# A banded attention and gated MLP kernel: a fourth staging buffer, 4 KB rows for two weights, and new lengths and margins in the planner that orders its instructions

## The chip, the cores and the metric

One core of one Trainium2 chip. The metric is the device time of one launch in microseconds. The kernel before takes 775.3 us (median of 3 runs, 772.66 to 777.56).

## What is computed

Attention over 4 batches, 8 heads, 768 positions and head width 64. A position sees itself and the 127 positions before it, and the first 4 positions of the sequence (the "sinks"). The result, 3072 rows of 512, goes through a gated MLP with 1536 hidden units. All is float32.

```python
scores = scale * np.matmul(q, k.transpose(0, 1, 3, 2))
keep = is_sink | in_window
scores = np.where(keep, scores, -1000000000.0)
scores = scores - np.max(scores, axis=-1, keepdims=True)
a = np.exp(scores)
a = a / (np.sum(a, axis=-1, keepdims=True) + 1e-09)
x = np.matmul(a, v)                      # then heads side by side: 3072 x 512
...
gate = 1.0 / (1.0 + np.exp(-(x @ w_gate)))
val = x @ w_val
return (gate * val @ w_out).astype(np.float32)
```

The three weights arrive as 64-bit floats.

## The kernel before, in words

**Tiling.** Attention runs in 96 units: a unit u is one head of one block of 256 query positions (`attend`, line 892). For each it forms scores on TensorE (PE), masks them and takes the maximum on VectorE (DVE), exponentiates on ScalarE (ACT), normalises (on GpSimd, ACT or DVE), turns the weights with PE transposes, cuts them into two triangular parts on GpSimd (POOL; `split`, `rest_of`) and multiplies by v. The first 20 units (`PLAIN`) use plain float32 matmuls of two passes; later ones split numbers into a high and a low part (tiles `hi`, `kl`, `vhl`) and use the faster fp32r form.

**The MLP** runs over 8 chunks of positions (`CHUNKS`), each over 12 slices f of 128 hidden units. Chunk 0 uses plain float32 (`feed_whole`, 1414), chunks 1 to 3 `feed_plain` (1515), and chunks 4 to 7, two blocks each, `feed_pair` (1561), which saves products by sums of blocks. Up products go to the PSUM tiles `m`, the down products to tiles `o` and `a`; between them stand `th`, `gh` and `gl` on ACT, DVE and POOL (`gated`, 1489).

**Weights.** `weights` (1307) calls `decode` (1256) 36 times: SP loads a 512 KB piece of 64-bit numbers into a staging tile `wst` (pool tag with `B_wst` = 3 buffers; the mask builder takes one of them first), and two ACT and two DVE instructions make float32 of it. `halves` (1334) and `thirds` (1343) split the weights in high and low parts; low parts are written to DRAM (`wlo_d`, `spare`, 1319) and read back slice by slice (`fetch`, 1462, tile `lo`, 8 buffers).

**The order of everything** is made at build time by a planner (`class Plan`, `run`, line 353). Each operation has a priority, the tiles it reads and writes, and one or more ways: an engine and a length in ns. `run` plays the program through with these lengths. Whenever an engine is free it gives it the first ready operation by priority; so the lengths decide which engine takes an operation that has several ways, and in what order each engine's instructions stand. Between the end of an operation and the readiness of one that needs it the planner puts `LAT` = 180 ns (line 411); PE first takes operations whose inputs are at least `SURE` = 600 ns old (`SURE_D` = 1200 ns for a landed DMA). Where PE has nothing ready in the first 130 us, `run` puts a filler, a 128x128 matmul of the identity (`warm`, 807; `m<-ident` in the trace; line 537). On the chip each engine then goes through its list in this order and waits on semaphores; the planner's lengths themselves are not waited for. All DMAs are issued by one queue, SP.

**The end.** The general branch for other masks is skipped by a jump. `hint` (1685) puts branch hints for PE, DVE and SP in their lists, called in `last_slice` (1641, the call is line 1665).

Line 620 is the helper that issues every planned instruction, so nearly all rows have L620.

Of the kernel before, what the change touches and what calls it, by code (L numbers as in the profile page):

```python
# [29 lines left out]
CROWD = 1.0  # L30
# [4 lines left out]
BACKV = 0.0  # L35
FLIP = 1
HOLD = 0.6
HELD = 800000.0
GAP = 2.0
# [3 lines left out]
THIRDS = 130000.0  # L43
CROWDED = 350000.0
PLAIN = 20
SINKP = -2.0
SCALP = -0.5
SKSWAP = 0
WHOLE = 1
DN1 = 36  # L50
DS1 = 8.0
DR1 = 0.2
DS2 = 18.0
DR2 = 0.3
KS1 = 16.0
KR = 0.9
KS2 = 25.0
XP = -900.0
ALT = 1
LAT = 180.0  # L60
BULK = 620.0
ISSUE = 550.0
SURE = 600.0
SURE_D = 1200.0
FREE = 150.0
NEXT = dict(PE=0.0, V=60.0, A=60.0, G=60.0, Q=0.0)
# [21 lines left out]
B_lo = 8  # L88
B_w2 = 2
B_wst = 3  # L90
# [222 lines left out]
class Plan:  # L313
# [39 lines left out]
    def run(self, warm, fill_ns, fill):  # L353
# [37 lines left out]
        while events:  # L391
            now = events[0][0]
            while events and events[0][0] <= now:
# [14 lines left out]
                for x in o.after:  # L408
                    x.before -= 1
                    same = len(x.ways) == 1 and x.ways[0][0] == on  # L410
                    x.ready = max(x.ready, now + (NEXT[on] if same else LAT))
                    if on != "PE":
                        x.sure = max(x.sure, now + LAT + (SURE_D if o.dma else SURE))
                    if not x.before:
                        n += 1
                        heapq.heappush(events, (x.ready, n, ("ready", x, None)))
            for e in free:
                if free[e] > now:
                    continue
                held = []  # L420
                unsure = [] if e == "PE" else None
                while waiting[e] or unsure:
# [18 lines left out]
                    if unsure is not None and (  # L441
                        o.sure > now
                        or any(slots[k][v - 1][1] + LAT + SURE > now for k, v in need.items())
# [51 lines left out]
                    if through:  # L495
                        ns += max(0.0, port - now - LEAD)
                        port = now + ns + (70.0 if e == "V" else 0.0)
# [26 lines left out]
                    for x in o.after:  # L524
                        x.todo -= 1
                        x.due = max(x.due, end + LAT)
# [23 lines left out]
def kernel(  # L550
# [13 lines left out]
    w_gate, w_val, w_out = (  # L564
        w.bitcast(I32).rearrange("r (c w) -> r c w", w=2) for w in (w_gate, w_val, w_out)
    )
    B, H, S, D = v.shape
    DM, DF, _ = w_gate.shape
    DO = w_out.shape[1]
    NC = DM // 128  # L570
    NF = DF // 128
# [63 lines left out]
    def act(cols, psum=False):  # L635
        return 120 + 0.9 * cols

    def pool(cols):
        return Port(170 + 2.17 * cols)
# [199 lines left out]
    WLO, LOADS, GROUPS, DECODED, READY, READY2 = (Fixed(None) for _ in range(6))  # L839

    def sinks(b, u):
        if not b:
# [7 lines left out]
            for t, x in enumerate(VS0):  # L850
                for y in range(2):
                    o = 64 * y + NS * t
                    dma(
                        u + 0.5, 91.0, lambda x=x, y=y, o=o: Q.dma_start(
# [8 lines left out]
        for o in range(0, 128, NS):  # L863
            dma(
                u, 91.0, lambda o=o: Q.dma_start(
                    out=raw()[o : o + NS], in_=v[b, :, 0:NS, :].rearrange("h p d -> p h d"),
                ), [READY2], [(raw, o)] + [VSHL[b, i] for i in range(2) if b and (b, i) in VSHL],
# [10 lines left out]
    def load(u, b, h, t0, T, prev, L, vraw, vin, qkT, plain):  # L878
# [4 lines left out]
            u, 0.75 * n * R / D, lambda: Q.dma_start(out=qkT()[0:R, 0:n], in_=qk[b, h, 0:R, c0 : c0 + n]),  # L883
# [3 lines left out]
            u, 100.0 * L, lambda: Q.dma_start(  # L887
# [4 lines left out]
    def attend(u, b, h, t0, T, XR):  # L892
# [44 lines left out]
        for t in range(T):  # L937
# [28 lines left out]
            def exp(t=t):  # L966
# [5 lines left out]
            plan.op(u, [("PE", 10 + (4 * n / 2.4 + 6 if plain else 2 * mac(n)), scores)], qk_reads, [sc, (P, t)], busy=0.5 if plain else 0.9)  # L972
            plan.op(
                u, [("V", 260 if first else 535, top)],
                [sc, (MASKS, 3), (MASKS, min(t0 + t, 2))], [sc, (P, t), (NEGM, (u, t))],
            )
            plan.op(u, [("A", 410, exp)], [], [(P, t), (rs, t)])
# [19 lines left out]
        def mul():  # L997
            for t in range(T):
# [4 lines left out]
                ("A", 200, lambda: A.activation(  # L1003
                    out=rs()[:, 0:T], in_=rs()[:, 0:T], func=AF.Copy, scale=1.0, bias=1.0e-9
                )),
                ("G", Port(213), guard(G)), ("V", Port(100), guard(V)),
# [3 lines left out]
            u, [("V", 110, lambda: V.reciprocal(out=rs()[:, 0:T], in_=rs()[:, 0:T]))], [], [rs]  # L1010
        )
        plan.op(u, [("G", Port(660), share), ("A", 720, mul), ("V", Port(555), scale)], [rs], [P])

        if not plain:
# [11 lines left out]
                u, [("V", 180, lambda: V.transpose(  # L1026
# [10 lines left out]
                u, [("G", Port(610), spread(G)), ("V", two(W), spread(V))], [turned, OWN], [sk]  # L1037
# [35 lines left out]
        plan.op(u, [("PE", 30 + (T + plain) * 110, turn)], [P], [tp, wt], busy=0.45)  # L1073
# [745 lines left out]
```

## Time and profile before

| | |
|---|---|
| runs | 775.3 us median (772.66, 775.3, 777.56) |
| the profiled execution, its own time | 774.19 us |
| its span, first to last instruction | 772.5 us |
| instructions | 16296 |
| TensorE clock granted, mean | 0.998 |
| DMA bytes | 185.57 MB, 240 GB/s over the span |

The page counts a matmul as busy from its start to a modelled end, and matmuls overlap: a wait shorter than what the last matmul's record still covers does not show as idle time. Rows with "[1.63 <-DMA x]" tell the idle time of the engine before the instruction and what ended it.

### The profile page before, as it was taken

To read this page: it belongs to the slowest core of one execution; us is meant where nothing else is said; L and a number is where in the kernel's file an instruction comes from. 1 tells how busy PE (TensorE), PEld (TensorE's weight loads), DVE (VectorE), ACT (ScalarE), POOL (GpSimd) and SP (SyncE) were. 2 spreads that over 40 slices of the span, in tenths; PEclk is the share of its full clock that TensorE was granted. 3 is DMA by queue.
4 is the path that set the end of the run, shared out by engine and by line. 5 is a ranking of instruction groups with operands and counts; after the bars stand their busy time and mean duration, and the time that the engine had idled before them with its cause. 6 is when DMAs were issued, how large, how long until landed. Compare 5 with 4: busy or idle time off the path is not lost.

```text
span 772.5 us, 16296 instructions
## 1 busy us (share of the span) xinstructions
PE 749.1 (97%) x4986; PEld 674.9 (87%) x4986; DVE 607.5 (79%) x1782; ACT 472.0 (61%) x1338; POOL 506.1 (66%) x647
## 2 busy tenths in 40 slices
PE   7999999999999999999999999999999999999995
PEld 6866777998989999989999988999999999999995
DVE  5979988996999999969988889778999884433333
ACT  7879888765765777737666665457776652322221
POOL 3654676887999999937777977557976855321210
PEclk9999999999999999999999999999999999999999
DMA  6898987999999877677767777867697655677662
GB/s 165 222 297 250 323 263 234 376 307 311 342 294 319 284 220 207 200 252 231 233 224 225 242 233 222 246 196 251 193 306 249 196 159 178 217 240 211 198 205 86
DMA packets 120879, 185.57 MB, mean 240 GB/s; under 512 B 23248, under 2 KB 45264, under 8 KB 120784
## 3 DMA queue, kind: packets, MB, share of 16 engines
q1 hardware_dynamic: 120784, 184.45, 75.9%
q8 instruction: 42, 0.69, 0.4%
q14 instruction: 53, 0.43, 0.2%
HBM read 159.24 MB, written 25.17 MB: 239 GB/s over the span
## 4 chain that ended last, share of the span: by engine, by line
PE 61%; DVE 11%; DMA 6%; POOL 3%; ACT 2%; issue 2%; SPq 0%; ACTq 0%; POOLq 0%; DVEq 0%
PE m L620 34%; PE a L620 16%; PE o L620 11%; DVE ws L620 2%; DMA wst<-in_moe_w_gate_dram 1%; DMA out_dram<-w 1%; DVE P L620 1%; DVE th L620 1%; DMA vraw<-in_vt_dram 1%; DMA lo<-wlo_d 1%; DVE vhl L620 1%; POOL wt L620 1%; DVE hi L620 1%; DVE gl L620 1%; DVE xf L620 1%
## 5 line engine op out<-in xcount | busy, mean ns | idle before, releaser
L620 PE MATMUL m<-ws,ws 128*128 128x256 f32 x1536 | 290.0, 284 | 0.6 <-DVE th L620 0.2
L620 PE MATMUL m<-ws,lo 128*128 128x256 f32 x1344 | 288.6, 283 | 1.9 <-DMA lo<-wlo_d 1.3
L620 PEld LDWEIGHTS m<-ws,ws 128*128 128x128 f32 x1536 | 244.9, 189 | 13.1 <-DVE th L620 1.0
L620 PEld LDWEIGHTS m<-ws,lo 128*128 128x128 f32 x1344 | 215.0, 189 | 3.1 <-DMA lo<-wlo_d 2.3
L620 POOL TENSOR_SCALAR_AFFINE_SELECT wt<-wt 128x512 fp32r<-128x512 f32 (+3 forms) x192 | 125.9, 657 | 43.5 <-DVE wt L620 18.7
L620 POOL TENSOR_TENSOR gl<-th,gh 128x512 fp32r<-128x512 f32 (+1 forms) x34 | 38.2, 1122 | 99.6 <-ACT gh L620 82.7
L620 ACT ACTIVATE P<-P,negm_all 128x144 f32<-128x144 f32 x192 | 78.9, 412 | 28.7 <-DVE negm_all L620 26.8
L620 ACT ACTIVATE th<-m 128x256 f32<-128x256 f32 x96 | 36.6, 382 | 75.5 <-DVE th L620 71.9
L620 DVE TENSOR_TENSOR cv<-m,cv 128x256 f32<-128x256 f32 x96 | 40.2, 418 | 52.4 <-ACT cv L620 34.8
L620 ACT CAST gh<-th 128x512 fp32r<-128x512 f32 (+1 forms) x82 | 42.9, 523 | 55.3 <-DVE th L620 53.7
L620 POOL TENSOR_TENSOR ws<-ws,ws 128x512 fp32r<-128x512 f32 (+1 forms) x53 | 66.6, 1262 | 9.8 <-DVE ws L620 6.9
L620 PE MATMUL o<-ws,gh 128*128 128x512 f32 x168 | 67.6, 403 | 0.0
L620 PE MATMUL o<-ws,gl 128*128 128x512 f32 x168 | 66.2, 394 | 0.0
L620 PE MATMUL o<-lo,gh 128*128 128x512 f32 x168 | 65.8, 391 | 0.0
L620 DVE CUSTOM_DVE_ANT_0 P<-a,am 128x144 f32<-128x144 f32 x192 | 58.3, 306 | 8.8 <-PE a L620 2.2
L620 PE MATMUL a<-wt,vhl 128*128 128x256 f32 (+2 forms) x282 | 61.0, 327 | 1.8 <-POOL wt L620 1.6
L620 POOL TENSOR_TENSOR kl<-qkT,hi 128x400 fp32r<-128x400 f32 (+1 forms) x56 | 59.2, 1057 | 1.8
L620 PEld LDWEIGHTS a<-wt,vhl 128*128 128x128 f32 x282 | 47.3, 189 | 10.5 <-POOL wt L620 4.1
L620 ACT CAST hi<-qkT 128x656 fp32r<-128x656 f32 (+1 forms) x70 | 49.2, 703 | 10.9 <-PE a L620 10.0
L620 POOL TENSOR_TENSOR P<-P,rs 128x288 f32<-128x288 f32 x46 | 35.1, 764 | 29.8 <-DVE rs L620 26.2
L620 POOL TENSOR_TENSOR hi<-qkT,hi 64x256 fp32r<-64x256 f32 x53 | 41.2, 777 | 14.9 <-issue 4.9
L620 DVE COPY_PREDICATED a<-tri,a 128x128 f32<-128x128 int32 x160 | 45.4, 284 | 3.5 <-PE a L620 3.2
(146 smaller groups left out, 1735.5 us busy)
## 6 DMA issues: line engine op xcount, KB each, us to landing
lo<-wlo_d SPq DMA_DIRECT2D x396, 256.0 KB, 3.7
wlo_d<-ws SPq DMA_DIRECT2D x72, 256.0 KB, 4.3
qkT<-in_qk_dram SPq DMA_DIRECT2D x52, 328.0 KB, 4.1
qkT<-in_qk_dram SPq DMA_DIRECT2D x24, 264.0 KB, 3.5
wst<-in_moe_w_gate_dram SPq DMA_DIRECT2D x12, 512.0 KB, 4.8
wst<-in_moe_w_val_dram SPq DMA_DIRECT2D x12, 512.0 KB, 5.1
wst<-in_moe_w_out_dram SPq DMA_DIRECT2D x12, 512.0 KB, 5.4
out_dram<-w SPq DMA_DIRECT2D x20, 256.0 KB, 4.4
```

What stands on the lines that cost most here:

```text
L620: return lambda *a, **kw: tc.keep_in_program_order(op(*a, **kw))
```

## The change

The table of planner constants is replaced. `B_wst` is 4. The single `LAT` gives way to `AFTER` (from the end of an operation to its signal, by engine) plus `TOLD` (from the signal to the start, by engine) plus a margin: `SLACK` 60 ns behind results, `DSLACK` 300 ns behind DMA landings; `SURE` is 900 and `SURE_D` 600. Lengths of operations are set anew (`act`, `pool`, exp, transposes and others), on DVE, ACT and POOL multiplied by `CROWD` 1.04 where it was 1.0. A DMA's length is worked out from its packets (`moved`), and the planner doesn't issue one when more than about 4 us of transfers are queued. `SPLIT` makes the planner put the splitting of chunk 2 and 3's inputs behind the splitting of the weights; on the chip it adds no semaphore. The host lays `moe_w_gate` and `moe_w_val` out so that a slice's load reads rows of 4 KB, where it read runs of 1 KB. The hint for the three engines is called six slices from the end.

```diff
-DS1 = 8.0
-DR1 = 0.2
+DS1 = 10
+DR1 = 0.25
...
-LAT = 180.0
-BULK = 620.0
-ISSUE = 550.0
-SURE = 600.0
-SURE_D = 1200.0
+AFTER = dict(PE=163.0, V=75.0, A=100.0, G=35.0, Q=0.0)
+TOLD = dict(PE=54.0, V=35.0, A=35.0, G=77.0, Q=27.0)
+REACH = 2000.0
+LANDED = 430.0
+SLACK = 60
+DSLACK = 300
+QUEUED = 4000
...
+SURE = 900
+SURE_D = 600
...
-B_wst = 3
+B_wst = 4
...
-                    x.ready = max(x.ready, now + (NEXT[on] if same else LAT))
+                    lat = AFTER[on] + TOLD[x.ways[0][0]] + (DSLACK if o.dma else SLACK)
+                    x.ready = max(x.ready, now + (NEXT[on] if same else lat))
...
+                if e == "Q" and dma_free > now + REACH + QUEUED:
+                    n += 1
+                    heapq.heappush(events, (dma_free - REACH - QUEUED, n, None))
                     continue
...
-                        slow = BULK if o.dma > 1000.0 else 0.0
-                        dma_free = max(dma_free + o.dma, end + 650 + slow + o.dma)
-                        end = dma_free + 750
+                        dma_free = max(dma_free, now + REACH) + o.dma
+                        end = dma_free + LANDED
...
     def act(cols, psum=False):
-        return 120 + 0.9 * cols
+        return 28 + 0.93 * cols
...
+    def moved(n, size):
+        return n * (16 + size / 24.0)
...
-                copy(u, W, hi, xv, read, [(H1, i), (L1, i)], plain)
+                copy(u, W, hi, xv, read + [SPLIT] * (ci > WHOLE + GUARD), [(H1, i), (L1, i)], plain)
...
-            decode(prio(), w[:, fs].rearrange("(c p) f w -> p c f w", p=128), whole)
+            decode(prio(), w[f], whole)
...
-        copy(pr, 512, hi, whole, [whole, *r], [hi, (lo, 0)], start=start)
+        copy(
+            pr, 512, hi, whole, [whole, *r], [hi, (lo, 0)] + [(SPLIT, (f, k))] * (k > 2), start=start
+        )
...
+        if ci == len(CHUNKS) - 1 and f == NF - 6:
+            hint([gh], [th], [wol])
         downs(pe, f, O, gh, gl, woh, wol, (1.3, 1.5, 1.65, 1.7))
...
-        hint([(gh, 1)], [(th, 1)], [wol])
...
+    for name in ("moe_w_gate", "moe_w_val"):
+        made[name] = inputs[name].reshape(4, 128, -1, 128).transpose(2, 1, 0, 3)
```

What this makes of the lists of instructions is shown at three places. First SP, from the load of the fourth unit's q and k (`qkT`, whose buffers rotate over three) to that of the sixth; `w` are sink rows of v in 32 KB pieces. Before:

```order
L620 DMA qkT_103<-in_qk_dram 64x528
L620 DMA kl_160<-in_vt_dram 128x2x64
L620 DMA qkT_121<-in_qk_dram 64x528
L620 DMA wst_197<-in_moe_w_gate_dram 128x4x256
L620 DMA wst_202<-in_moe_w_val_dram 128x4x256
L620 DMA wst_209<-in_moe_w_out_dram 128x1024
L620 DMA w_215<-in_v_dram 16x8x64 x3
L620 DMA qkT_165<-in_qk_dram 64x528
```

And with the change:

```order
L630 DMA qkT_103<-in_qk_dram 64x528
L630 DMA wst_183<-in_moe_w_gate_dram 128x1024
L630 DMA wst_188<-in_moe_w_val_dram 128x1024
L630 DMA qkT_121<-in_qk_dram 64x528
L630 DMA wst_198<-in_moe_w_out_dram 128x1024
L630 DMA wst_204<-in_moe_w_gate_dram 128x1024
L630 DMA w_215<-in_v_dram 16x8x64 x4
L630 DMA qkT_155<-in_qk_dram 64x528
```

The fifth unit's load (`qkT_121`) now stands behind two 512 KB loads, where it stood before all of them, and the sixth unit's (the last row) behind four, where it stood behind three.

Second PE, from the fillers ahead of the third unit's transposes (`a<-ident,P`) to the sixth unit's scores (`a<-qkT_165`, now `a<-qkT_155`, 144 and 272 columns). Before:

```order
L620 MATMUL m_91<-ident 128x128 x3
L620 MATMUL a_278<-ident,P_231 128x128 x2
L620 MATMUL a_278<-ident,P_231 32x128
L620 MATMUL m_91<-ident 128x128
L620 MATMUL a_287<-qkT_121 128x144
L620 MATMUL a_289<-qkT_121 128x272
L620 MATMUL a_296<-ident,P_246 128x128 x2
L620 MATMUL a_296<-ident,P_246 32x128
L620 MATMUL m_91<-ident 128x128
L620 MATMUL a_309<-qkT_165 128x144
L620 MATMUL a_314<-qkT_165 128x272
```

And with the change, beginning behind the third unit's transposes:

```order
L630 MATMUL a_293<-qkT_121 128x144
L630 MATMUL a_295<-qkT_121 128x272
L630 MATMUL m_91<-ident 128x128 x5
L630 MATMUL a_321<-wt_297,vhl_134 128x256
L630 MATMUL a_321<-wt_297,vhl_134 128x128
L630 MATMUL m_91<-ident 128x128 x2
L630 MATMUL a_338<-ident,P_252 128x128 x2
L630 MATMUL a_338<-ident,P_252 32x128
L630 MATMUL m_91<-ident 128x128
L630 MATMUL a_346<-qkT_155 128x144
L630 MATMUL a_349<-qkT_155 128x272
```

Between the fifth unit's scores and the sixth unit's stood one filler; now eight stand there, and the third unit's first product with v has moved ahead of them. In the whole list the fillers go from 26 to 44; the other PE instructions are the same in number.

Third PE at the thirteenth unit, in chunk 0's MLP: its transposes (`a<-ident,P_674` before, `P_704` after) and its product with v (`a<-wt_760` before, `wt_766` after), with up products (`m`) and down products (`o`) about them. Before:

```order
L620 MATMUL a_749<-ident,P_674 128x128 x2
L620 MATMUL a_749<-ident,P_674 32x128
L620 MATMUL m_92<-hi_270,ws_605 128x256 x2
L620 MATMUL a_768<-qkT_165 128x272
L620 MATMUL a_772<-qkT_165 128x272
L620 MATMUL m_92<-xf_423,ws_605 128x256 x2
L620 MATMUL a_785<-ident,P_699 128x128 x2
L620 MATMUL a_785<-ident,P_699 32x128
L620 MATMUL a_790<-wt_760,vhl_116 128x256
```

And with the change:

```order
L630 MATMUL a_756<-ident,P_704 128x128 x2
L630 MATMUL a_756<-ident,P_704 32x128
L630 MATMUL a_718<-wt_724,kl_152 128x256
L630 MATMUL a_718<-wt_724,kl_152 128x128 x2
L630 MATMUL a_718<-sk_129,vshl_118 128x128
L630 MATMUL a_718<-sk_129,vshl_123 128x128
L630 MATMUL a_775<-qkT_155 128x272
L630 MATMUL a_783<-qkT_155 128x272
L630 MATMUL o_645<-ws_421,th_650 128x512
L630 MATMUL o_662<-ws_421,th_650 128x512
L630 MATMUL a_800<-wt_766,vhl_116 128x256
```

More columns of other work now stand between the transposes and the product that needs their cut result. Beyond these places, the instructions of DVE, ACT and POOL change engine here and there: `gl` at full width goes from 22 to 37 on POOL and from 25 to 10 on DVE; the normalising of `P` on ACT from 78 to 104 instructions, on DVE from 22 to 6, on POOL from 46 to 41. In all DVE's list gets 67 instructions shorter, ACT's 54 and POOL's 18 longer. Most of PE's operations stand within ten places of where they stood.

## Rows read from the trace of the kernel before

**Rows 1.** The page, busy time by engine: us, share of span, instructions.

```profile
PE 749.1 (97%) x4986; PEld 674.9 (87%) x4986; DVE 607.5 (79%) x1782; ACT 472.0 (61%) x1338; POOL 506.1 (66%) x647
```

**Rows 2.** Busy time by stretch: width, PE, PEld, DVE, ACT, POOL, clock, DMA, GB/s.

```profile
0.00:25.00 25.00, 19.75 (x120) 17.58 (x121) 15.55 (x78) 19.52 (x57) 11.29 (x30) 1.00 0.63 160
25.00:50.00 25.00, 23.43 (x126) 18.61 (x126) 20.72 (x70) 20.95 (x54) 14.98 (x23) 1.00 1.01 275
50.00:130.00 80.00, 76.72 (x352) 56.97 (x350) 71.47 (x185) 71.06 (x137) 45.87 (x54) 1.00 0.86 269
130.00:250.00 120.00, 118.37 (x823) 107.93 (x823) 105.49 (x268) 77.88 (x233) 107.59 (x127) 1.00 0.96 323
250.00:480.00 230.00, 226.53 (x1598) 209.92 (x1598) 205.82 (x649) 149.91 (x475) 182.21 (x241) 1.00 0.74 231
480.00:600.00 120.00, 119.99 (x846) 111.98 (x845) 104.56 (x323) 77.72 (x239) 86.89 (x115) 1.00 0.75 238
600.00:750.00 150.00, 149.84 (x1043) 139.17 (x1043) 76.98 (x200) 50.78 (x137) 55.99 (x61) 1.00 0.65 201
```

**Rows 3.** The chain that ended last, late in the program: start, us, what.

```profile
652.03 2.87 PE m L620 x24
```

**Rows 4.** Groups of instructions on PE: busy us, mean ns, idle before.

```profile
L620 PE MATMUL m<-ws,ws 128*128 128x256 f32 x1536 | 290.0, 284 | 0.6 <-DVE th L620 0.2 <-ACT th L620 0.2
...
L620 PE MATMUL m<-ident 128*128 128x128 f32 x52 | 9.9, 317 | 1.4 <-POOL ident masks.py:199 1.4
```

**Rows 5.** Who PE waited for, 25 to 480 us: total, times, longest.

```profile
PE a L620 <- POOL wt L620: 1.8, 4, 0.6
PE a L620 <- POOL P L620: 1.4, 3, 0.6
PE m L620 <- DMA lo<-wlo_d: 1.3, 2, 1.0
...
PE m L620 <- DVE th L620: 0.2, 1, 0.2
```

**Rows 6.** PE at the start, in order of time: start, us, instruction.

```profile
6.53 1.05 PE L620 MATMUL m<-ident 128*128 128x128 f32 x8
9.49 0.55 PE L620 MATMUL a<-ident,P 128*128 128x128 f32 x3 [1.91 <-POOL P L620]
...
18.34 0.94 PE L620 MATMUL a<-qkT 128*128 128x144 f32 x4 [1.63 <-DMA qkT<-in_qk_dram]
```

**Rows 7.** SP at the start: the first weight load, the sixth unit's load.

```profile
8.71 0.59 SPq L620 DMA_DIRECT2D wst<-in_moe_w_gate_dram  x1
...
11.91 0.47 SPq L620 DMA_DIRECT2D qkT<-in_qk_dram  x1
```

**Rows 8.** DMA issues by line: KB each, median us to landing.

```profile
wst<-in_moe_w_gate_dram SPq DMA_DIRECT2D x12, 512.0 KB, 4.8
...
wst<-in_moe_w_out_dram SPq DMA_DIRECT2D x12, 512.0 KB, 5.4
```

**Rows 9.** PE at the thirteenth unit's product with v.

```profile
59.99 1.14 PE L620 MATMUL a<-wt,vhl 128*128 128x256 f32 x6 [0.57 <-POOL wt L620]
```

**Rows 10.** ACT's group that first reads a landed weight.

```profile
L620 ACT ACTIVATE ws<-wst 128x512 f32<-128x512 f32 x35 | 24.0, 685 | 9.4 <-DMA wst<-in_moe_w_val_dram 5.4 <-DMA wst<-in_moe_w_gate_dram 2.1 <-DMA wst<-in_moe_w_out_dram 1.7
```

**Rows 11.** POOL's group of `gl` at full width.

```profile
L620 POOL TENSOR_TENSOR gl<-th,gh 128x512 fp32r<-128x512 f32 x22 | 28.5, 1295 | 97.4 <-ACT gh L620 80.6 <-DVE gh L620 10.9 <-DMA lo<-wlo_d 5.1
```

**Rows 12.** The normalising of P on DVE, alone and beside a POOL subtraction.

```profile
58.45 0.48 DVE L620 TENSOR_SCALAR P<-P,rs 128x144 f32<-128x144 f32 x2
...
66.94 2.67 POOL L620 TENSOR_TENSOR ws<-ws,ws 128x512 fp32r<-128x512 f32 x2
...
67.35 2.36 DVE L620 TENSOR_SCALAR P<-P,rs 128x144 f32<-128x144 f32 x2
```

**Rows 13.** The end: the four last stores on SP, the last copy on DVE.

```profile
764.11 3.48 SPq L620 DMA_DIRECT2D out_dram<-xf  x4
...
764.96 0.42 DVE L620 TENSOR_SCALAR xf<-o 128x256 f32<-128x256 f32 x1 [0.28 <-ACT xf L620]
```

More of the change, by code (lines that the diff above doesn't have):

```diff
@@ L442, in run @@
                         o.sure > now
-                        or any(slots[k][v - 1][1] + LAT + SURE > now for k, v in need.items())
+                        or any(slots[k][v - 1][1] + AFTER["V"] + TOLD["PE"] + SURE > now for k, v in need.items())
                     ):
@@ L496, in run @@
                         ns += max(0.0, port - now - LEAD)
-                        port = now + ns + (70.0 if e == "V" else 0.0)
+                        port = now + ns + AFTER[e]
                     if e == "PE":
@@ L525, in run @@
                         x.todo -= 1
[L526 removed]
+                        x.due = max(x.due, end + AFTER[e] + TOLD[x.ways[0][0]])
                         if not x.todo and x.ways[0][0] in soon:
@@ L838 @@
     X0 = {}
-    WLO, LOADS, GROUPS, DECODED, READY, READY2 = (Fixed(None) for _ in range(6))
+    WLO, SPLIT, GROUPS, DECODED, READY, READY2 = (Fixed(None) for _ in range(6))
     def sinks(b, u):
@@ L864, in sinks @@
             dma(
-                u, 91.0, lambda o=o: Q.dma_start(
+                u, moved(8, 256), lambda o=o: Q.dma_start(
                     out=raw()[o : o + NS], in_=v[b, :, 0:NS, :].rearrange("h p d -> p h d"),
-                ), [READY2], [(raw, o)] + [VSHL[b, i] for i in range(2) if b and (b, i) in VSHL],
+                ), [READY2], [(raw, o)] + [(VSHL[b, i], o) for i in range(2) if b and (b, i) in VSHL],
             )
@@ L886, in load @@
         dma(
-            u, 100.0 * L, lambda: Q.dma_start(
+            u, moved(8 * L, 256) if plain else moved(8, 256 * L), lambda: Q.dma_start(
                 out=vin(), in_=vt[b, h, :, k0 // 128 : k0 // 128 + L]
@@ L970, in exp @@
                 )
-            plan.op(u, [("PE", 10 + (4 * n / 2.4 + 6 if plain else 2 * mac(n)), scores)], qk_reads, [sc, (P, t)], busy=0.5 if plain else 0.9)
+            plan.op(u, [("PE", (10 + 4 * n / 2.4 + 6 if plain else 249 if n > 256 else 177), scores)], qk_reads, [sc, (P, t)], busy=0.5 if plain else 0.9)
             plan.op(
-                u, [("V", 260 if first else 535, top)],
+                u, [("V", 222 if first else 545, top)],
                 [sc, (MASKS, 3), (MASKS, min(t0 + t, 2))], [sc, (P, t), (NEGM, (u, t))],
             )
-            plan.op(u, [("A", 410, exp)], [], [(P, t), (rs, t)])
+            plan.op(u, [("A", 405, exp)], [], [(P, t), (rs, t)])
         def guard(E):
@@ L1036, in attend @@
             plan.op(
-                u, [("G", Port(610), spread(G)), ("V", two(W), spread(V))], [turned, OWN], [sk]
+                u, [("G", Port(568), spread(G)), ("V", two(W), spread(V))], [turned, OWN], [sk]
             )
@@ L1071, in rest_of @@
             )
-        plan.op(u, [("PE", 30 + (T + plain) * 110, turn)], [P], [tp, wt], busy=0.45)
+        plan.op(u, [("PE", 20 + T * 60 + 190 * plain, turn)], [P], [tp, wt], busy=0.45)
         plan.op(
@@ L1262, in decode @@
         hw = lambda: st()[:, :, :, 1]
-        plan.op(prio, [("Q", ISSUE, lambda: Q.dma_start(out=st(), in_=src))], [], [st], dma=1456.0)
+        plan.op(prio, [("Q", ISSUE, lambda: Q.dma_start(out=st(), in_=src))], [], [st], dma=moved(8, 8 * n * m))
         by = lambda i: st().rearrange("p n m w -> p (n m w)").bitcast(U16).rearrange(
@@ L1320, in spare @@
         dma(
-            pr, 728.0, lambda: Q.dma_start(
+            pr, moved(8, 2048), lambda: Q.dma_start(
                 out=wlo_d[f, :, k * 512 : k * 512 + 512],
@@ L1390, in out_tiles @@
                 plan.op(-1000.0 + ci + 1, ways if last else ways[:1], [acc], [ot])
-            dma(ci, 728.0, lambda ot=ot, r=r: Q.dma_start(out=out[r : r + 128], in_=ot()), [ot])
+            dma(ci, moved(8, 2048), lambda ot=ot, r=r: Q.dma_start(out=out[r : r + 128], in_=ot()), [ot])
     def feed(ci):
```

59 lines of the change are left out of this document (31 added, 28 removed).

## The prediction

> **What bounds the kernel now.** I read the page's busy times first: PE is busy 97% of the span, the next engine 79% [rows 1]. So PE is the bound, and the change adds no product and takes none away; it can win only time in which PE waits. Then I read the busy times by stretch [rows 2]. PE's idle time, the width less its first number, is 5.25 us up to 25 us, 1.57 up to 50, 3.28 up to 130, 1.63 up to 250, 3.47 up to 480, and after that 0.01 and 0.16. From 480 us to the last products there is nothing to win.
>
> The busy time flatters PE. The chain of work that ended last shows 24 products of 256 columns in 2.87 us [rows 3], 120 ns each, while a record of one counts 284 ns [rows 4]. A wait that follows such a product is thus hidden by up to 164 ns.
>
> Third, the waits of PE between 25 and 480 us [rows 5]: 12 rows with 22 waits and 9.3 us in all, spread over POOL's cut weights and normalised scores, DMA landings, ACT and DVE. No row holds more than 1.8 us. So no single edit takes much away; the ceiling for the middle of the program is the 9.95 us of idle time there (1.57 + 3.28 + 1.63 + 3.47) and up to 22 x 0.164 = 3.6 us hidden behind records, 13.6 us together.
>
> At last the start [rows 6]: PE waits 1.91 us for the first normalised scores and 1.63 us for the sixth unit's q and k, and between them it runs fillers.
>
> **The change part by part.** The sum is made against the profiled execution, 774.2 us (span 772.5), which is 1.1 us under the median of the runs, 775.3.
>
> *Lengths and margins.* These move no work off PE; they change how much other work stands between a producer and PE's use of it. The place shown is the thirteenth unit: its product with v waited 0.57 us for POOL's cut [rows 9], since one up product in halves, two scores and another unit's transposes did not cover the way over ACT and POOL. Now another unit's second product, two scores and two down products stand there, and the down products are 512 columns wide. That wait should go. Elsewhere the order differs little: most PE operations stand within some ten places of where they stood. I take half of the ceiling, 6.8 us, as gained. Bounds: all of it, 13.6 us, and below nothing, since a new order makes new waits: as many again as now, +9.3 us by [rows 5]. Half is my choice, because the 22 waits are short and have many causes, and some will come back elsewhere.
>
> *Fillers and the start.* In the lists the fillers go from 26 to 44. The trace holds two records for each (52) [rows 4]; eight records took 1.05 us [rows 6], 0.13 each. So 18 more cost 18 x 2 x 0.13 = 4.7 us if they push real work back, and nothing if they lie in waits. There is room: 5.25 us of idle time stand in the first 25 us [rows 2]. But the load order adds a wait of its own. The sixth unit's load was issued at 11.91 us, behind three 512 KB loads issued from 8.71 us [rows 7], and PE was idle 1.63 us for its landing [rows 6]. Now a fourth such load stands ahead of it. The core moved 275 GB/s in the stretch with full DMA queues [rows 2], so 0.524 MB take 1.9 us: that wait grows from 1.63 to about 3.5 us, and the new fillers stand right in front of it, so the two aren't added. The first transposes' wait of 1.91 us stays, as the lists begin alike. What the earlier load of the second slice's gate weights brings back is work ready sooner, in the stretch of 25 to 130 us, and is in the 6.8 us above. I take +2.0 us for the start, nearest to the 1.9 us of one load; bounds: 0 and +4.7, and on the other side -1.6, the whole present wait, if the landing order matters less than it seems.
>
> *4 KB rows and the fourth buffer.* The third weight has come in 4 KB rows all along, and it lands 5.4 us after its issue, the gate weight in 1 KB runs 4.8 us [rows 8]. No row says that the layout lands sooner. PE waits for no staging tile [rows 5]; ACT does, 9.4 us in all before its first reading instruction [rows 10], in the stretch where ACT is busy 71.06 of 80 us [rows 2]. The cover is the decoding ahead of PE's need. I take 0; bounds: nothing, and -3.3 us, all of PE's idle time from 50 to 130 us. If the cover were gone, ACT's wait would come through at most one for one, +9.4 us.
>
> *Work between engines.* DVE gives about 15 full-width `gl` to POOL, at 1.295 us each there [rows 11]: 19.4 us more on an engine that has 182 of 230 us in the middle stretch [rows 2]. Even with all of it there it would be at 88%. The last of a slice's three down products alone needs `gl`, and POOL waited 97.4 us before that group [rows 11], so it is hidden. ACT takes 26 more normalisings; it has 80 us free in that stretch [rows 2]. I take 0; the price if the cover goes is the rival on POOL below.
>
> *The hint.* DVE's last copy ends at 765.4 us (764.96 + 0.42), and SP goes on issuing the four last stores until 767.6 (764.11 + 3.48) [rows 13]. One store takes about 0.87 us of that, so a queue held up by nothing would end its issues at 766.3: 1.3 us could be won, if it is the hint in its present place that holds SP. If the jump's target is no longer at hand so long after the hint, something may be lost instead; no row prices it, and I bound it by the same 1.3 us. I take 0.
>
> *Sum.* 774.2 + 2.0 - 6.8 = 769.4; with the 1.1 us of the median, 770.5 us, 0.6% under before. About 1% (7.8 us) is what a measurement of this kernel can tell from no change, so my forecast is: within 1%, on the fast side. Its own range, with the middle's gain between 3 and 10 us, is 767 to 774.
>
> **The rivals.**
>
> *The waits were mostly the wrong lengths' doing.* If the planner now knows what the chip takes, three quarters of the 13.6 us go, and the fillers lie in waits: 774.2 - 10.2 = 764.0, 1.3 more from the end is 762.7, and the median is 763.8. For it: the waits of [rows 5] are all of one kind, PE a little too early for a result, which a truer table cures at once. Against it: the lists of PE are much alike, and the start has gained fillers.
>
> *No gain.* The waits only change place and the start costs its 2.0 us: 776.2, the median 777.3. For it: the waits are many and small. Against it: the margins behind a result are longer than the 180 ns, which puts more PE work in front of each use.
>
> *Slower: POOL holds DVE up.* DVE's normalising of one unit took 0.48 us alone, and 2.36 us where POOL was in two subtractions of 2.67 us [rows 12]: 1.88 us lost on the way to PE's transposes. Every full-width `gl` put on POOL lays 1.295 us more in DVE's way. If in one of two such cases, some 8 of 15, the held-up DVE instruction stands on a unit's way to PE and PE's cover is gone, PE waits 8 x 1.88 = 15 us; with half of the middle's gain lost besides (3.4 left of 6.8) and the start's 2.0, this is 774.2 + 15 - 3.4 + 2 = 787.8, the median 789. It decides from 3 such waits on: 3 x 1.88 = 5.6 us outweigh the 4.8 us that the sum would have won. Against it: DVE's list is 67 instructions shorter, and its own normalising, the kind that was held up, goes from 22 instructions to 6.
>
> The Trainium skill's page "SBUF — State Buffer", in "Who interferes with whom", speaks against the change here: a DVE instruction with two SBUF inputs, or in a two-port mode, and a GpSimd instruction that reads SBUF exclude each other for the whole of an instruction, and the second one blocks. The trace agrees: the 2.36 us instruction pair above ends with POOL's. By that rule each `gl` moved to POOL blocks such DVE work for its full length; it is the last rival above, and the sum by it would be that rival's.
>
> **How the numbers follow.** I give the forecast 0.43, the fast rival 0.33, no gain 0.10, the slow rival 0.14. Of the forecast's own range a small part (0.03) lies under 767.5, 1% below before: faster by over 1% is 0.33 + 0.03 = 0.36. Slower by over 1% (783) is 0.14. The rest, 0.40 + 0.10, is within 1%: 0.50. The range that should hold 8 in 10 goes from 761, a little below the fast rival, to 780, between no gain and the slow rival, whose half is left out.
>
> **What would show it.** Right: PE's idle time from 25 to 480 us falls from 9.95 to about 5 us; 88 filler records in the place of 52; the sixth unit's scores still wait for a DMA at the start, and longer; POOL's busy time rises by 15 to 30 us and DVE's falls by about as much; weight loads land no sooner. Wrong: PE's idle time in the middle unchanged or up, with POOL's or DVE's products as what ended it (the slow rival); or the first 25 us with less idle time than now in spite of more fillers, and the middle under 3 us (the fast one).

## The result, and the profile after

The changed kernel takes 765.95 us (median of 4 runs, 765.86 to 766.14), beside 774.98 us for the kernel before on the same chip: ratio 0.9883, 95% interval 0.9851 to 0.9915. It is faster by 1.2% (0.9 to 1.5). Measured once more among the experiments it took 765.45 us (0.9887, 0.9857 to 0.9917); the trace of that run is the second trace below. The profiled execution took 766.04 us, its span is 764.3 us, 8.2 less than before.

The page's busy times, which answer to [rows 1], and its line on DMA packets:

```profile
PE 745.7 (98%) x5022; PEld 680.2 (89%) x5022; DVE 586.9 (77%) x1715; ACT 485.2 (63%) x1392; POOL 532.8 (70%) x665
...
DMA packets 111661, 185.55 MB, mean 243 GB/s; under 512 B 23248, under 2 KB 32976, under 8 KB 111568
...
PE 84%; DVE 7%; POOL 3%; ACT 2%; issue 1%; DMA 1%; POOLq 0%; ACTq 0%; DVEq 0%
```

The last two of these lines on the page of before:

```profile
DMA packets 120879, 185.57 MB, mean 240 GB/s; under 512 B 23248, under 2 KB 45264, under 8 KB 120784
...
PE 61%; DVE 11%; DMA 6%; POOL 3%; ACT 2%; issue 2%; SPq 0%; ACTq 0%; POOLq 0%; DVEq 0%
```

PE has 36 more records than before (5022 for 4986), all fillers. DVE lost 20.6 us of work, POOL gained 26.7. There are 120784 - 111568 = 9216 fewer packets, 384 for each of the 24 loads whose 1 KB runs became 4 KB rows. The last line, the chain that ended last, is PE's for 84% of the span, where it was 61%.

Busy times by stretch, in the columns of [rows 2]:

```profile
0.00:25.00 25.00, 20.13 (x126) 18.02 (x127) 15.95 (x80) 19.97 (x55) 11.00 (x28) 1.00 0.64 177
25.00:50.00 25.00, 21.64 (x122) 18.01 (x121) 15.90 (x51) 18.04 (x49) 15.52 (x19) 0.93 0.92 246
50.00:130.00 80.00, 80.00 (x382) 62.81 (x381) 71.41 (x187) 75.99 (x167) 51.45 (x60) 1.00 0.89 283
130.00:250.00 120.00, 118.42 (x840) 110.14 (x839) 107.95 (x273) 80.25 (x235) 109.74 (x128) 1.00 0.94 318
250.00:480.00 230.00, 228.79 (x1629) 213.96 (x1629) 198.54 (x632) 164.92 (x526) 198.53 (x258) 1.00 0.75 236
480.00:600.00 120.00, 120.00 (x851) 112.20 (x850) 101.62 (x317) 79.89 (x249) 98.43 (x129) 1.00 0.77 241
600.00:750.00 150.00, 150.00 (x1047) 139.86 (x1046) 71.37 (x172) 43.73 (x111) 48.07 (x48) 1.00 0.63 199
```

Read the counts beside the times. In the first 50 us PE has 248 records, 88 of them fillers (all stand there), so 160 of real work; before it had 246, 52 of them fillers, so 194. From 50 to 130 us it has 382 for 352. The changed kernel falls back at the start and catches up. From 130 to 600 us it has 840 + 1629 + 851 = 3320 records for 823 + 1598 + 846 = 3267. At 470 us / 3320 = 0.142 us a record, these 53 are, by estimate, 7.5 us of work done earlier. (The records are not all alike; with each weighted by the usual distance from one start to the next for its shape, the estimate is 7.6.) But PE's idle time in these three stretches fell only from 1.63 + 3.47 + 0.01 = 5.11 to 1.58 + 1.21 + 0.00 = 2.79 us, by 2.3. The other 5.2 us never showed as idle time, since a product's record covers a gap behind it [rows 3, 4]; that these gaps were waits is inferred. In the second trace of the changed kernel the same sums give 46 records more, 6.5 us, and 2.1 us less idle time. From 480 us on, where hardly any idle time was left before, there are still 851 + 1047 = 1898 records for 1889. The Trainium skill's page "Perfetto Trace Analysis", in "Summary: the profiler window per engine type", says that a TensorE record ends at an estimated end; the counts here fit that, since idle time between records does not hold all that was won.

The output stores give a like picture in another way. The view of the tensor `out_dram` lists its stores with the start of the first and of the last; the 20 stores of the first seven chunks, then the 4 of the last chunk. Before:

```profile
L620 SPq DMA_DIRECT2D out_dram<-w x20: 337/341/425, 132.5 to 679.6; - x20
L620 SPq DMA_DIRECT2D out_dram<-xf x4: 338/654/1547, 764.1 to 766.9; - x4
```

After:

```profile
L630 SPq DMA_DIRECT2D out_dram<-w x20: 337/368/747, 134.3 to 670.3; - x20
L630 SPq DMA_DIRECT2D out_dram<-xf x4: 338/394/1572, 756.0 to 758.6; - x4
```

And in the second trace of the changed kernel:

```profile
L630 SPq DMA_DIRECT2D out_dram<-w x20: 337/338/461, 133.5 to 670.5; - x20
L630 SPq DMA_DIRECT2D out_dram<-xf x4: 338/394/1394, 756.2 to 758.5; - x4
```

The first store, at the end of the first chunk, stands 1.8 us later (132.5, 134.3). From there to the first store of the last chunk it took 631.6 us before and 621.7 after: 9.9 us won. Start and middle together are the 8.1 us; the tail, from that store to the end of the span, is 8.4 and 8.3 us. The border between start and middle is known to about 1 us: with the same lists the second trace puts it at 133.5, so 1.0 us lost and 8.9 won. And at 130 us PE is only 4 records of real work behind in the first trace, and 4 ahead in the second.

PE's waits from 25 to 480 us, which answer to [rows 5]; there are 8 in all, where 22 were:

```profile
PE a L630 <- ACT P L630: 2.9, 1, 2.9
PE o L630 <- ACT w L630: 1.0, 1, 1.0
PE a L630 <- DVE sk L630: 0.5, 1, 0.5
PE o L630 <- ACT gh L630: 0.4, 1, 0.4
PE m L630 <- POOL ws L630: 0.4, 1, 0.4
PE a L630 <- DVE xf L630: 0.3, 1, 0.3
PE o L630 <- POOL gl L630: 0.3, 1, 0.3
PE a L630 <- DVE negm_all L630: 0.2, 1, 0.2
```

The first row is new. ACT and then PE at that place, in order of time (start, us, instruction, idle time before it and what ended it):

```profile
30.41 0.66 ACT L630 ACTIVATE ws<-wst 128x512 f32<-128x512 f32 x1 [3.71 <-DMA wst<-in_moe_w_out_dram]
30.97 0.70 ACT L630 ACTIVATE P<-P,rs 128x144 f32<-128x144 f32 x2
...
31.42 0.74 PE L630 MATMUL a<-ident,P 128*128 128x128 f32 x3 [2.91 <-ACT P L630]
...
33.48 2.85 PE L630 MATMUL a<-qkT 128*128 128x272 f32 x6 [0.45 <-DVE sk L630]
```

The second slice's `w_out` had not landed when ACT came to it. The normalising that PE's transposes needed stood behind it in ACT's list, so PE waited as well. After that the granted clock fell to the lower of its two levels (1.2 for 2.4 GHz) for a while; busy times by stretches of 2 us:

```profile
28.00:30.00 2.00, 0.51 (x4) 0.21 (x2) 0.00 (x0) 0.00 (x0) 1.68 (x2) 1.00 1.08 236
30.00:32.00 2.00, 0.58 (x4) 0.40 (x4) 0.43 (x1) 1.59 (x4) 0.00 (x0) 1.00 1.08 272
32.00:34.00 2.00, 1.55 (x9) 1.23 (x8) 0.79 (x4) 1.90 (x5) 0.74 (x3) 0.63 0.92 299
34.00:36.00 2.00, 2.00 (x6) 1.44 (x5) 0.91 (x4) 1.52 (x5) 1.93 (x4) 0.51 0.21 64
36.00:38.00 2.00, 2.00 (x15) 1.86 (x14) 1.24 (x6) 1.55 (x6) 1.15 (x1) 1.00 0.82 228
```

The thirteenth unit's wait for POOL's cut [rows 9] is gone from the list, as forecast, and so are the three others for such a cut.

### The profile page after: what moved, and what is told of

Same layout as the page of the kernel before. It is cut to its first block, busy times and chain, and to the rows that moved or that the text cites. A ratio compares the mean times of both kernels' runs of the same rounds, so it can differ in the third digit from the quotient of the medians.

```text
span 764.3 us, 16366 instructions
## 1 busy us (share of the span) xinstructions
PE 745.7 (98%) x5022; PEld 680.2 (89%) x5022; DVE 586.9 (77%) x1715; ACT 485.2 (63%) x1392; POOL 532.8 (70%) x665
## 2 busy tenths in 40 slices
DMA packets 111661, 185.55 MB, mean 243 GB/s; under 512 B 23248, under 2 KB 32976, under 8 KB 111568
## 3 DMA queue, kind: packets, MB, share of 16 engines
q1 hardware_dynamic: 111568, 184.45, 75.8%
## 4 chain that ended last, share of the span: by engine, by line
PE 84%; DVE 7%; POOL 3%; ACT 2%; issue 1%; DMA 1%; POOLq 0%; ACTq 0%; DVEq 0%
PE m L630 45%; PE a L630 24%; PE o L630 15%; DVE ws L630 2%; DMA wst<-in_moe_w_out_dram 1%; POOL ws L630 1%; DVE th L630 1%; DVE vhl L630 1%; DVE xf L630 1%; ACT P L630 1%; DVE P L630 1%; DVE gl L630 0%; POOL wt L630 0%; DVE sk L630 0%; DVE low L630 0%
## 5 line engine op out<-in xcount | busy, mean ns | idle before, releaser
L630 POOL TENSOR_SCALAR_AFFINE_SELECT wt<-wt 128x512 fp32r<-128x512 f32 (+3 forms) x192 | 119.4, 623 | 31.3 <-ACT wt L630 14.0
L630 POOL TENSOR_TENSOR gl<-th,gh 128x512 fp32r<-128x512 f32 (+1 forms) x49 | 57.4, 1171 | 95.1 <-ACT gh L630 86.2
L630 POOL TENSOR_TENSOR ws<-ws,ws 128x512 fp32r<-128x512 f32 (+1 forms) x57 | 73.1, 1294 | 6.3 <-DVE ws L630 3.2
L630 POOL TENSOR_TENSOR kl<-qkT,hi 128x400 fp32r<-128x400 f32 (+1 forms) x64 | 68.0, 1062 | 2.4
L630 POOL TENSOR_TENSOR hi<-qkT,hi 64x256 fp32r<-64x256 f32 x60 | 47.8, 796 | 20.4 <-DVE hi L630 5.3
L630 POOL TENSOR_TENSOR P<-P,rs 128x288 f32<-128x288 f32 x41 | 31.1, 760 | 29.6 <-DVE rs L630 23.3
```

What stands on the lines that cost most here:

```text
L630: return lambda *a, **kw: tc.keep_in_program_order(op(*a, **kw))
```

## The experiments

Each run is compared with runs of the kernel before on the same chip; those medians lie from 772.3 to 773.8 us. All kernels are planned anew unless it is said that the order stayed.

| run | us, median | ratio to before, 95% | first store of chunk 0 | of the last chunk |
|---|---|---|---|---|
| the changed kernel again | 765.45 | 0.9887 (0.9857 to 0.9917) | 133.5 | 756.2 |
| 1 KB runs again | 766.23 | 0.9917 (0.9892 to 0.9941) | 134.2 | 756.1 |
| hint at its old place | 767.16 | 0.9922 (0.9895 to 0.9949) | 134.9 | 756.7 |
| one decoding later | 765.92 | 0.9918 (0.9897 to 0.9940) | 132.5 | 755.0 |
| later still | 765.00 | 0.9881 (0.9857 to 0.9906) | 133.5 | 755.6 |
| before, 4 buffers and 4 KB rows | 780.61 | 1.0092 (1.0065 to 1.0119) | 137.0 | 771.5 |
| changed, 3 buffers | 772.60 | 0.9990 (0.9970 to 1.0009) | 138.3 | 761.0 |
| changed, old priorities | 782.08 | 1.0111 (1.0079 to 1.0142) | 135.1 | 771.0 |
| changed, no margins | 769.52 | 0.9933 (0.9913 to 0.9953) | 128.9 | 760.8 |
| changed, margins from 150 us on | 763.34 | 0.9875 (0.9842 to 0.9908) | 127.0 | 751.8 |
| changed, 61 ns for 60 | 769.73 | 0.9955 (0.9932 to 0.9977) | 134.9 | 760.5 |
| before, 181 ns for 180 | 779.35 | 1.0056 (1.0028 to 1.0085) | 135.4 | 769.7 |

The first store's time comes from one profiled execution each; two traces of the changed kernel differ by 0.8 us in it (134.3, 133.5).

**The changed kernel again.**

> The changed kernel itself, so that it stands among the same runs as the others: 765 to 767 us; the kernel before 771 to 776.

It came out as expected, and stands for the changed kernel in what follows.

**The layout alone.** The order of every engine stayed.

```diff
...
-            decode(prio(), w[f], whole)
+            decode(prio(), w[:, fs].rearrange("(c p) f w -> p c f w", p=128), whole)
...
-    for name in ("moe_w_gate", "moe_w_val"):
-        made[name] = inputs[name].reshape(4, 128, -1, 128).transpose(2, 1, 0, 3)
```

> The changed kernel with the gate and val weights laid out again in runs of 1 KB; the order of every engine is the same, instruction for instruction. Theory 'plan' (the gain lies in the order that the planner's numbers make, the layout is worth nothing): 765.4 to 766.6 us, within 0.6 us of the changed kernel's 766.0. Theory 'transfers' (a good part of the gain of 9 us comes from weights that land sooner): 769 us or more, and the gate and val loads land some 0.5 us or more later, which ACT's waits for staging tiles show.

766.23 us, 0.8 more than the changed kernel, with intervals that overlap: no difference that these runs show. The loads with 1 KB runs, KB each and median us to landing:

```profile
wst<-in_moe_w_gate_dram SPq DMA_DIRECT2D x12, 512.0 KB, 6.1
wst<-in_moe_w_val_dram SPq DMA_DIRECT2D x12, 512.0 KB, 5.6
```

and with 4 KB rows, in the changed kernel:

```profile
wst<-in_moe_w_gate_dram SPq DMA_DIRECT2D x12, 512.0 KB, 5.8
wst<-in_moe_w_val_dram SPq DMA_DIRECT2D x12, 512.0 KB, 5.3
```

With the same lists, longer rows landed 0.3 us sooner in these traces, and PE waits for the same eight results in both. Beside the kernel before [rows 8] the gate weights land later (4.8, 5.8). Why is not shown: in the run below with four decoding steps moved, the rest of the lists being the same, they landed in 4.8 us again, so 0.3 us is less than a small change of order makes. The Trainium skill's page "DMA: Bandwidth & Descriptors", in "Specifications", asks for at least 512 bytes in a transfer for full rate; both layouts have that for the weights, and by that no gain was due. The kernel's time agrees.

**The hint alone.** The lists are nearly the same.

```diff
-        if ci == len(CHUNKS) - 1 and f == NF - 6:
-            hint([gh], [th], [wol])
...
+        hint([(gh, 1)], [(th, 1)], [wol])
         high = gh, (lambda: woh()[:, 0], lambda: wol())
```

> The changed kernel with the branch hint at its old place, in the last slice; the lists are otherwise nearly the same. If the hint's place is worth nothing: 765.4 to 766.6 us, SP's issue of the second last output store takes 1.55 us in both. If the early hint saves SP's queue something: 767 us or more, and the last stores' issues begin or end later by that.

767.16 us, 1.7 more than the changed kernel, with intervals that overlap; the layout's run and the next one, on the same chip, lie 0.9 and 1.2 under it. It is also in the range that was expected if the early hint saves something, so the time alone doesn't decide it. Only the end could differ by the hint, and from the first of the last four stores to the end of the span it took 765.4 - 756.7 = 8.7 us, for 764.3 - 756.0 = 8.3. The longest of the four store issues took 1.95 us here, 1.57 in the changed kernel, 1.55 before, and 1.39 in the changed kernel's second trace, so it varies by itself. The stores of this run:

```profile
L630 SPq DMA_DIRECT2D out_dram<-xf x4: 338/576/1946, 756.7 to 759.6; - x4
```

So neither the layout nor the hint makes a good part of the 8 to 9 us; a microsecond or two of the hint's can't be excluded. What is left of the change acts through the lists: the planner's numbers, the fourth buffer, `SPLIT`.

**The new wait at the start.** Three decoding instructions of the second `w_out` were put later in the finished order; in the second run later still, with the fourth.

```diff
         self.time = now
+        at = {o.seq: i for i, (o, _, _) in enumerate(order) if o}
+        late = [at[34], at[35], at[36]]
+        moved = [order[i] for i in late]
+        to = order[at[37]]
+        order = [x for i, x in enumerate(order) if i not in late]
+        i = order.index(to)
+        order[i:i] = moved
```

> The changed kernel with one weight's three decoding instructions (of the second slice's w_out) moved behind the attention work that stood behind them on ACT and DVE; nothing else is moved. In the changed kernel ACT waits 3.71 us for that weight's landing at 26.7 us, PE then waits 2.91 us behind ACT at 31.4 us and its clock falls to half for 3.4 us. Theory 'PE sets the pace of the first 131 us': the wait and the slow clock go and come through at the end: 766.0 - 2.9 - 1.7 = 761.4 us, 761 to 763. Theory 'the decoding on ACT (76 of 80 us busy from 50 to 130 us) sets the end of that stretch': the wait goes, the first chunk's products end at the same time, and the run takes 765 to 767 us.

The wait at 31.4 us went and the clock stayed full, but PE waited later instead, behind ACT, which waited for a copy that stood behind a decoding step on DVE:

```profile
38.87 0.52 PE L637 MATMUL a<-ident,P 128*128 128x128 f32 x3 [3.06 <-ACT wt L637]
```

So the run did not tell the theories apart. The next one moved each step singly:

```diff
         self.time = now
+        seq = lambda x: x[0].seq if x[0] else None
+        for who, behind in ((34, 347), (35, 34), (36, 41), (37, 576)):
+            x = next(x for x in order if seq(x) == who)
+            order.remove(x)
+            i = next(i for i, y in enumerate(order) if seq(y) == behind)
+            order.insert(i + 1, x)
```

> As the run with one weight's decoding put later, but put later still and its last step with it: there the wait of 2.9 us at 31.4 us had only changed its place (3.06 us at 38.9 us, behind DVE's last decoding step). Theory 'PE sets the pace of the first 131 us': without either wait 761 to 763 us. Theory 'ACT's decoding sets the end of that stretch': the first chunk's products end no sooner, 765 to 767 us.

765.00 us; 0.5 less than the changed kernel among the same runs, and within their spread. Neither long wait is there, but PE's idle time from 25 to 50 us is 25 - 21.84 = 3.16 us, where it was 3.36: other results were late in turn. The stretch, and then the waits:

```profile
25.00:50.00 25.00, 21.84 (x128) 17.51 (x127) 16.97 (x57) 18.52 (x50) 16.72 (x21) 1.00 0.96 252
```

PE's waits from 25 to 480 us in the same run:

```profile
PE a L636 <- DMA qkT<-in_qk_dram: 1.6, 1, 1.6
PE o L636 <- ACT w L636: 1.0, 1, 1.0
PE m L636 <- DVE xf L636: 0.8, 1, 0.8
PE a L636 <- POOL wt L636: 0.6, 1, 0.6
```

Taking the wait of 2.9 us away was thus worth nothing that these runs show, and as other waits came in its place, the two theories stay undecided here. Mending one wait in a start in which several results are late moves the wait.

**The buffer and the numbers apart.** The first is the old planner with four buffers and the new layout, the second the new planner with three buffers.

```diff
-B_wst = 3
+B_wst = 4
...
```

> The kernel before, with the old planner, and of the change only the fourth staging buffer and the rows of 4 KB. Theory 'transfers': it makes most of the gain, 766 to 769 us. Theory 'plan': within 3 us of the kernel before, 772 to 778 us; the fourth buffer lets the old planner draw another order, so a few us to either side are open. PE's idle time from 25 to 480 us stays near 10 us.

780.61 us, 8 more than before, the opposite of what the theory on transfers asked for, and above the 772 to 778 us of the other. PE's idle time grew in three stretches: 80 - 75.31 = 4.69 us, 4.94 and 3.31.

```profile
50.00:130.00 80.00, 75.31 (x346) 56.09 (x345) 69.81 (x181) 68.90 (x146) 48.29 (x57) 1.00 0.92 293
130.00:250.00 120.00, 115.06 (x788) 103.92 (x789) 110.45 (x277) 77.54 (x230) 105.33 (x125) 1.00 0.90 298
...
480.00:600.00 120.00, 116.69 (x819) 108.29 (x818) 95.75 (x289) 66.89 (x207) 85.21 (x109) 1.00 0.72 227
```

```diff
-B_wst = 4
+B_wst = 3
```

> The changed kernel with three staging buffers in the place of four, planned anew. The old planner with the fourth buffer and the 4 KB rows took 780.6 us, 8 more than the kernel before of the same runs. Theory 'the numbers make all the gain and the buffer none': 764 to 768 us. Theory 'the fourth buffer costs time at the start, and the numbers make up for it': 758 to 763 us, with less idle time of PE in the first 50 us than the 8.2 us of the changed kernel. Theory 'the new plan needs the buffer': over 769 us, and ACT or PE wait longer for weights from 25 to 130 us.

772.60 us: all of the gain is gone, and the first store stands at 138.3 us, 4 us later than in the changed kernel. That is the range of the theory that the new plan needs the buffer. ACT's waits for weights from 25 to 130 us are only a little longer (5.4 us for 4.6). What stands out are fillers, 116 records for 88, 36 of them after 50 us, where the changed kernel has none: the planner had nothing ready for PE there.

```profile
L630 PE MATMUL m<-ident 128*128 128x128 f32 x116 | 18.8, 296 | 1.4 <-POOL ident masks.py:199 1.4
```

In these two plans neither the buffer nor the numbers brought the gain alone. Each is one order out of many, and the last experiment shows how much that alone can move.

**The old priorities with the new lengths.**

```diff
...
-HOLD = 0.8
+HOLD = 0.6
...
-GAP = 1.0
+GAP = 2.0
...
-KS1 = 17
-KR = 1.0
+KS1 = 16.0
+KR = 0.9
```

> The changed kernel with the old priorities and holding rules (CROWD, HOLD, GAP, THIRDS, SINKP, DS1, DR1, KS1, KR) and the new lengths, margins and DMA model. Theory 'lengths and margins bring the gain': 764 to 768 us. Theory 'they need the retuned priorities': 769 us or more.

782.08 us, 16 more than the changed kernel, three times what one nanosecond moves below. In this plan the new lengths win nothing with the old priorities.

**The margins.**

```diff
-SLACK = 60
-DSLACK = 300
+SLACK = 0
+DSLACK = 0
```

> The changed kernel with the margins behind results and landings (60 and 300 ns) at 0, planned anew: the lengths from the trace alone are left. Theory 'the margins bring the gain': 770 to 775 us, PE's waits from 25 to 480 us back at about 20 (22 before, 8 in the changed kernel). Theory 'the lengths bring it': 764 to 768 us and some 10 waits.

769.52 us, between the two ranges. PE has 10 waits from 25 to 480 us, as the theory on lengths asked. The first store is 5.4 us earlier than in the changed kernel (128.9 for 134.3), and the gain is lost from 130 to 250 us, where PE has 800 records for 840 and 4.71 us of idle time for 1.58:

```profile
130.00:250.00 120.00, 115.29 (x800) 106.21 (x801) 103.49 (x273) 81.87 (x235) 112.14 (x127) 0.99 0.95 319
```

That led to the next run, margins from 150 us of the plan's time on:

```diff
-                    lat = AFTER[on] + TOLD[x.ways[0][0]] + (DSLACK if o.dma else SLACK)
+                    lat = AFTER[on] + TOLD[x.ways[0][0]] + (DSLACK if o.dma else SLACK) * (now > 150000.0)
```

> The changed kernel with its margins (60 and 300 ns) used only from 150 us of the plan's own time on, and none before. Without any margin the kernel was 5.7 us ahead of the changed one when the first chunk ended, at about 131 us, lost it again by 200 us and ended 4 us behind. Theory 'margins cost at the start and pay later, and what is gained in a stretch stays': 760 us, 758 to 762. Theory 'each plan is a new draw, and the stretches don't add': 763 to 771 us.

```profile
L630 SPq DMA_DIRECT2D out_dram<-w x20: 337/338/415, 127.0 to 666.1; - x20
L630 SPq DMA_DIRECT2D out_dram<-xf x4: 338/395/1575, 751.8 to 754.3; - x4
```

763.34 us, the lowest median of all. It lies at the low end of what was expected if each plan is a new draw, and above the 758 to 762 if stretches add. The profiled execution (761.9) was the lowest of its six. In it the first store is 7.3 us earlier than in the changed kernel, and the last chunk's first store still 4.2 us earlier (751.8 for 756.0). So the first chunk can end earlier with as much decoding on ACT, which speaks against the theory that ACT sets the end of that stretch, and in this trace more than half of the lead lasts to the end. Over all runs it is 2.1 us under the changed kernel (765.45), and the two intervals overlap almost wholly, so that it beats the changed kernel is not shown.

**How far one draw of a plan moves the time.** A planner with the same rules can come to many orders; each is called a draw here. One nanosecond, in the new planner and in the old:

```diff
-SLACK = 60
+SLACK = 61
```

> The changed kernel with the margin behind results at 61 ns in the place of 60, planned anew: a step that changes no rule, but some hundreds of places in the lists. It shows how far the draw of a plan alone moves the time. If little: 764.5 to 767 us. If the draw decides as much as the numbers: anywhere from 761 to 773 us, and the gain of 9 us can't be put down to the margins or the lengths alone.

```diff
-LAT = 180.0
+LAT = 181.0
```

> The kernel before with its latency constant at 181 ns in the place of 180, planned anew; all else is old. It shows whether the 773 to 775 us of the kernel before stand for its rules or for one draw of them. If they stand for the rules: 771 to 777 us, and the new rules' two draws (765.5 and 769.7) are both faster than either of the old. If the draw decides: 778 us or more, or 769 or less, and the two families of plans overlap.

769.73 us, 4.3 more than the changed kernel with an interval that lies above its own; and 779.35 us, 5.5 more than the kernel before of the same runs. Neither step changes a rule, but both change most of the order: fillers aside, compared place by place, the traces have another product, by tile and shape, at 3019 of PE's 4934 places for the first step and at 2983 for the second, nearly as many as between the two kernels (3443). So two draws of one family lie 4 to 6 us apart here, and each kernel that was compared is the better of its two. Old 773.8 and 779.4, new 765.5 and 769.7: the new pair lies 9 us lower in the mean, and its worse draw is under the better of the old. With two draws each this speaks for the new version's plans and doesn't settle it; and the runs with three buffers, old priorities and no margins, one draw each, can't put the gain down to one constant.

## Why the prediction was right and wrong

The forecast was 770.5 us, within 1% on the fast side; 765.95 lies in the range, 4.5 us under the forecast and 2.2 over the fast rival's 763.8. The likeliest case was "within 1%"; the measured one is "faster by over 1%", with an interval that reaches down to 0.9%. The middle came out near the fast rival's 10.2 us, the start nearer to the forecast's.

- **The middle, -6.8 us, was mis-sized; it measured -9.9** between the first store and the last chunk's (-8.9 in the second trace). The ceiling of 13.6 us was not passed, but its hidden part was put too low: "22 x 0.164 = 3.6 us hidden behind records", and half of that, 1.8, in the sum. It counted only the waits that the list of waits names. But a gap of under 164 ns behind any of some 3300 products in that stretch is no wait in the list at all. Of the 7.5 us won from 130 to 600 us, 5.2 were of that kind (4.4 of 6.5 in the second trace). For the same reason "From 480 us to the last products there is nothing to win" was wrong: 9 records, some 1.3 us by estimate, were won there. The mechanism, more PE work between a result and its use, fits the waits, 8 for 22; that the margins made it is not shown, since without them there were 10.
- **The start, +2.0 us, measured +1.8 at the end of the first chunk** (+1.0 in the second trace), but not by the steps given; the close fit is luck. The fillers are 88 records, as forecast. The sixth unit's load was issued at 13.9 us in the place of 11.9. Its scores do not wait, where the forecast had them wait longer: they start at 19.79 us for 18.34, with 16 filler records between them and the fifth unit's, and the seventh unit's scores wait. What had not been seen is that PE stands 34 records of real work behind at 50 us, and gets 30 of them back by 130 us. Two larger errors of opposite sign made a right sum. PE at this place:

```profile
19.79 0.94 PE L630 MATMUL a<-qkT 128*128 128x144 f32 x4
...
22.87 0.94 PE L630 MATMUL a<-qkT 128*128 128x144 f32 x4 [1.24 <-DMA qkT<-in_qk_dram]
```

- **Staging, 0.** With identical lists the rows of 4 KB are worth less than the runs can show. But the cover that the text named, "the decoding ahead of PE's need", was gone at 30 us: ACT's wait for a landing came through to PE almost whole (3.71, 2.91). Moving that wait away won nothing measurable. Of the 9.4 us that ACT waited before, 6.7 lay in the stretch from 50 to 130 us, not all. The fourth buffer's own worth could not be told from the draw of the plan.
- **Work between engines, 0, shows no cost**: POOL +26.7 us and DVE -20.6, and 15 more `gl` of full width on POOL (37 for 22), which cost PE one wait of 0.3 us from 25 to 480 us. The group on POOL, which answers to [rows 11], stands below. The slow rival did not come: PE waited for DVE three times from 25 to 480 us, 1.0 us together, where the rival needed 5.6. No run put this work back by itself.
- **The hint, 0, stands as far as the runs can tell**: with the hint at its old place the end took 0.4 us more in one trace, which is less than the 1.3 us of the bound. That bound took 0.87 us, the mean of four, for a store's issue; the single issues took 0.34 to 1.55 us.
- **What would show it.** PE's idle time from 25 to 480 us went from 9.95 to 3.36 + 0 + 1.58 + 1.21 = 6.15 us, not to 5, and yet more time was won than forecast; the sign that was to be looked at misses the hidden part. Of the fast rival's two signs one came, less idle time in the first 25 us (4.87 for 5.25), and the other, under 3 us in the middle, did not.

```profile
L630 POOL TENSOR_TENSOR gl<-th,gh 128x512 fp32r<-128x512 f32 x37 | 47.9, 1295 | 94.3 <-ACT gh L630 86.0 <-DVE gh L630 6.3 <-PE m L630 1.3
```

What no term covered is the draw. The forecast argued from rules to places, as if the plan were a smooth function of its numbers; one nanosecond changes most places of PE's list and moves the time by 4 to 6 us, which is more than every term but one. That the total lies in the range is therefore in part luck as well.

## What to carry to other kernels

Where the records of the engine that bounds the kernel overlap, count its instructions in a stretch beside its busy time: the idle time alone showed less than a third of what was won from 130 to 600 us here. Before a retuned scheduler constant is credited with a gain, plan once more with a neighbouring value in both versions, and compare the spread with the gain. When one wait at a busy start is removed and nothing comes of it, look at what was late next before mending another.

## What was not expected of the hardware

- After a stretch of 4 us in which PE was busy 0.51 and 0.58 of each 2 us, the granted clock fell to 0.63 and 0.51 in the two next, so to 1.2 GHz for most of the first and nearly all of the second, and was back at 1.00 (2.4 GHz) after that. Six score products took 2.85 us in it, 0.48 each; in the run with the decoding put later still, four of the same shape took 1.16 us, 0.29 each, and there the clock stayed at 1.00 although PE had been busy only 0.43 of 2 us from 30 to 32 us, between two full stretches. The four products, and busy times of that run:

```profile
31.74 1.16 PE L636 MATMUL a<-qkT 128*128 128x272 f32 x4 [1.57 <-DMA qkT<-in_qk_dram]
...
28.00:30.00 2.00, 2.00 (x16) 1.63 (x14) 0.78 (x4) 1.25 (x4) 1.92 (x3) 1.00 1.09 268
30.00:32.00 2.00, 0.43 (x2) 0.29 (x2) 0.61 (x3) 1.39 (x5) 1.86 (x5) 1.00 1.05 253
32.00:34.00 2.00, 2.00 (x14) 1.79 (x14) 1.14 (x6) 0.79 (x4) 1.74 (x2) 1.00 1.09 341
```

- One of the four last stores takes SP 0.87 to 1.95 us to issue in every kernel traced, wherever the hint stands; what holds it was not found.
